# Sigmoid attention with a GELU feed-forward layer: raw weights and a parked intermediate move to GpSimd's DMA queue, three loads move to the next stage, and the first stage decodes one weight unit less

## The chip, the cores and the metric

One core of a Trainium2 chip runs the kernel. The metric is the device time of one execution in microseconds (us).

## The reference

```
scores = q @ k^T / 8 - ln(448)             # 8 batches, 12 heads, 448 tokens, 64 channels
x = sigmoid(scores) @ v                     # laid out as [8*448 tokens, 12*64 = 768 channels]
h = x @ w_in                                # w_in 768 x 2048
out = (0.5 * h * (1 + erf(h / sqrt(2)))) @ w_out   # w_out 2048 x 768
```

Everything is float32 at the interface except the two weight matrices, which lie in DRAM as 64-bit floats: the kernel turns them into 32-bit floats itself ("decodes" them).

## The kernel before

**Batches and tokens.** The eight batches are taken in the order 7, 0, 1, ... 6. The attention output of the first one is parked in DRAM (`scr_x`), and its 448 tokens are dealt out, 64 each, to the seven others. So the feed-forward layer runs seven times over 512 tokens (448 + 64).

**Stages.** `attention_first` computes the first two batches' attention, 12 head pairs, with nothing else for TensorE. Then come seven rounds of `ffn1(t)` (the first product, GELU) and `window(t + 2, t)`, in which the second product of round t is interleaved with the attention of a later batch. The first three batches ("plain", `PLAIN = 3`) multiply 32-bit floats directly; later ones and all feed-forward products use float32r, each operand split into a high and a low part (`xh`/`xl`, `whl`, `g`).

**Order.** The schedule is written out by hand: an engine executes its instructions in the order in which the program issues them, and a DMA queue issues its transfers in that order too. Each of SyncE's (`nc.sync`) and GpSimd's (`nc.gpsimd`) instruction streams is one such queue.

**A plain head pair n.** `load_plain(n)` issues four transfers on SyncE's queue, 704 KB in all: q (224 KB), k in two halves (112 KB each), v (256 KB). In `attention_first` pair n + 3 is loaded after the values of pair n - 1, into buffers that earlier pairs have left. `scores_plain` issues two score products (L340) for each of four key chunks and a sigmoid on ScalarE (L314) after each; `values_plain` multiplies with v (L356), copies the result (ScalarE L365) and subtracts (VectorE L366). For the first batch the two results go to `scr_x` (L368, L369) on SyncE's queue.

**Decoding.** `decoder()` is a generator that is advanced by `W.decode(n)`, n in chunks, two steps to a chunk. A chunk is one unit of w_in (768 KB raw) or half a unit of w_out (512 KB raw). `load(i)` fetches the raw chunk into one of three places in turn (two halves of `raw_ring`, one tile `raw`). Step one of iteration i runs `start(i)`: three VectorE instructions (L117, L119, L122) that wait for the raw load. Step two runs `scale(i)`: two ScalarE instructions (L130, L133), then for the chunk before it `end(i - 1)`: two VectorE instructions (L138, L147), and then `load(i + 2)`, which goes into the place that L138 has just finished reading. With L117, L119 and L138 all in program order between the sigmoids and casts of the attention, a late raw chunk holds VectorE, then ScalarE (L130), and then the sigmoid for which TensorE waits.

The pace of decoding is set by three numbers of chunks: `PACE_A` over `attention_first`, `PACE_F` over `ffn1(0)`, `PACE_W` over `window(2, 0)`. There are 40 chunks (16 of w_in, 24 of w_out). The call in the first stage is

```
for c in range(4):
    scores_plain(n, c)
    W.decode(PACE_A * (4 * n + c - 3) / (4 * total - 4))     # total = 12
```

Decoded w_in units are stored on SyncE's queue during `ffn1(0)` and decoded w_out units on GpSimd's (L190), for the later rounds to read back.

Of the kernel before, what the change touches and what calls it, by code (L numbers as in the profile page):

```python
# [9 lines left out]
F32 = mybir.dt.float32  # L10
# [3 lines left out]
I64 = mybir.dt.int64  # L14
# [8 lines left out]
def tile_sigmoid_attention_gelu_ffn(  # L23
# [11 lines left out]
    nc = tc.nc  # L35
    B, NPAIR, _, S = q.shape
# [28 lines left out]
    def g_tile(fc, name, dtype=F32R):  # L65
        return const.tile([P, 2, T], dtype, tag=f"g{fc}", name=name)
# [3 lines left out]
    scr_x = tc.dram_tile([2, P, NPAIR, S], F32, name="scr_x")  # L70
# [1 line left out]


    PLAIN = 3
    PACE_A, PACE_F, PACE_W = 14, 8, 24
    SUB_IN, SUB_OUT = NC * P, NFH * P // 2
    SUB = max(SUB_IN, SUB_OUT)
    KEPT = 4
# [5 lines left out]
    def width(kind):  # L84
        return (NC if kind == "in" else NFH) * P

    def decoder():


        chunks = [  # L90
            (kind, u, c0, sub)
            for kind, u in UNITS
            for sub in (SUB_IN if kind == "in" else SUB_OUT,)
            for c0 in range(0, width(kind), sub)
        ]
        raws, parts = {}, {}
        raw_ring = sb.tile([P, 2, 2 * SUB], U32, tag="raw", name="raw_ring", bufs=1)
        me_ring = sb.tile([P, 2, 2, SUB], U32, tag="me", name="me_ring", bufs=1)

        def load(i):  # L100
            if i >= len(chunks):
                return
            kind, u, c0, w = chunks[i]
            src = (w_in if kind == "in" else w_out)[u].rearrange("p a b -> p (a b)")
            if i % 3 < 2:
                raw = raw_ring[:, i % 3]
            else:
                raw = sb.tile([P, 2 * SUB], U32, tag="a", name=f"raw{i}", bufs=1)
            raw = raw[:, : 2 * w]
            nc.sync.dma_start(raw.bitcast(I64), src[:, c0 : c0 + w])  # L110
            raws[i] = raw.rearrange("p (n t) -> p n t", t=2)

        def start(i):
            w = chunks[i][3]
            low, high = raws[i][:, :, 0], raws[i][:, :, 1]
            m, e = me_ring[:, i % 2, 0, :w], me_ring[:, i % 2, 1, :w]
            nc.vector.tensor_scalar(e, high, 0x7FF00000, None, op0=ALU.bitwise_and)  # L117

            nc.vector.tensor_scalar(  # L119
                m, high, 11, 0x80000000, op0=ALU.logical_shift_left, op1=ALU.bitwise_or  # L120
            )
            nc.vector.scalar_tensor_tensor(  # L122
                m, low, 21, m, op0=ALU.logical_shift_right, op1=ALU.bitwise_or
            )
            parts[i] = m, e

        def scale(i):

            e = parts[i][1]
            nc.scalar.activation(  # L130
                e.bitcast(F32), e.bitcast(I32), AF.Relu, bias=1151.0 * 2**23, scale=-8.0
            )
            nc.scalar.activation(e, e.bitcast(F32), AF.Relu, bias=255.0 * 2**23, scale=-1.0)  # L133

        def end(i):
            high = raws.pop(i)[:, :, 1]
            m, e = parts.pop(i)
            nc.vector.scalar_tensor_tensor(  # L138
                e, high, 0x80000000, e, op0=ALU.bitwise_and, op1=ALU.bitwise_or
            )  # L140
            kind, u, c0, w = chunks[i]
            if c0 == 0 and kind == "in":
                first_w[kind, u] = g_tile(u, f"w_in{u}", F32).rearrange("p a b -> p (a b)")
            elif c0 == 0:
                first_w[kind, u] = sb.tile([P, WU], F32, tag="wst", name=f"w_out{u}", bufs=WST)
            t = first_w[kind, u][:, c0 : c0 + w]
            nc.vector.scalar_tensor_tensor(  # L147
                t, m, 2.0**-31, e.bitcast(F32), op0=ALU.mult, op1=ALU.mult
            )

        load(0)
        load(1)
        yield False
        for i in range(len(chunks) + 1):
            if i == 0:
                load(2)
            if i < len(chunks):
                start(i)
                yield False
                scale(i)  # L160
            if i > 0:
                end(i - 1)
                load(i + 2)
            yield i > 0 and chunks[i - 1][2] + chunks[i - 1][3] == width(chunks[i - 1][0])
# [77 lines left out]
    def rows(j):  # L242
        return slice(j * D, j * D + D)
# [72 lines left out]
    def load_plain(n):  # L316

        b, hp = divmod(n, NPAIR)
        if b >= PLAIN:
            return  # L320
        if n % 3 < 2:
            qk = sb.tile([P, 2, S], F32, tag="kr", name=f"qk{n}")
            qr, kr = qk[:, 0], qk[:, 1]
        else:
            qr, kr = (sb.tile([P, S], F32, tag="qr", name=f"{x}r{n}") for x in "qk")
        nc.sync.dma_start(qr, q[(b - 1) % B, hp])
        for j in range(2):
            nc.sync.dma_start(kr[rows(j)], k[(b - 1) % B, hp, rows(j), j])  # L328
        vr = sb.tile([P, 2, 4, D], F32, tag=("vr", "vs")[n % 2], name=f"vr{n}")
        nc.sync.dma_start(vr, v[(b - 1) % B, hp])  # L330
        raws[n] = qr, kr, vr
# [17 lines left out]
    def values_plain(n):  # L349
        b, hp = divmod(n, NPAIR)  # L350
        vr = raws.pop(n)[2]
        pav = ps_av.tile([P, 512], F32, tag="pav", name=f"pav{n}")
        for c in range(4):
            a = attn.pop((n, c))
            for j in range(2):
                nc.tensor.matmul(  # L356
                    pav[rows(j), :S], vr[:, j, c], a[:, j], start=c == 0, stop=c == 3
                )
        if b > 0:
            th, tl = xh[:, hp, :S], xl[:, hp, :S]  # L360
        else:
            th, tl = (
                sb.tile([P, S], F32R, tag="tmp", name=f"x{n}{b}_{hp}", bufs=3) for n in "hl"
            )
        nc.scalar.copy(th, pav[:, :S])  # L365
        nc.vector.tensor_tensor(tl, pav[:, :S], th, op=ALU.subtract)  # L366
        if b == 0:
            nc.sync.dma_start(scr_x[0, :, hp], th.bitcast(F32))  # L368
            nc.sync.dma_start(scr_x[1, :, hp], tl.bitcast(F32))  # L369

    def load_tokens(t):

        for n, x in enumerate((xh, xl)):
            nc.sync.dma_start(x[:, :, S:].bitcast(F32), scr_x[n, :, :, t * TOK : (t + 1) * TOK])
# [23 lines left out]
    def attention_first():  # L398

        total = 2 * NPAIR  # L400
        load_plain(0)
        load_plain(1)
        W.decode(0)
        load_plain(2)
        for n in range(total):
            for c in range(4):
                scores_plain(n, c)
                W.decode(PACE_A * (4 * n + c - 3) / (4 * total - 4))
            if n > 0:
                values_plain(n - 1)  # L410
            load_plain(n + 3)
            if n == NPAIR + 2:
                load_tokens(0)
            W.prepare_to(min(n - total + 3, 2))
        values_plain(total - 1)
# [17 lines left out]
    def ffn1(b):  # L433
        for fc in range(NF):
            if b == 0:
                W.store_to(fc + 3)
            if (b, fc) not in phs:
                hidden(b, fc, range(NC - 1))
            W.prepare_to(W.pos[b, "in", fc] + (2 if b == 0 else AHD))
            ph = hidden(b, fc, range(NC - 1, NC))  # L440
            if b == 0:
                W.prepare_to(W.pos[b, "in", fc] + 3)
            g[fc] = g_tile(fc, f"g{b}_{fc}")
            gf = sb.tile([P, T], F32, tag="tmp", name=f"gf{b}_{fc}", bufs=3)
            nc.scalar.activation(gf, ph, AF.Gelu)  # L445
            nc.scalar.activation(g[fc][:, 0], ph, AF.Gelu)  # L446
            nc.vector.tensor_tensor(g[fc][:, 1], gf, g[fc][:, 0], op=ALU.subtract)  # L447
            if b > 0:
                W.prepare_to(W.pos[b, "in", fc] + AHD + 1)
            if b + 2 >= PLAIN:  # L450
                if fc in (NF - 10, NF - 8):
                    load_pair(b + 2, (fc - NF + 10) // 2)
                if fc in (NF - 4, NF - 2):
                    split_head(b + 2, (fc - NF + 4) // 2)
                if fc == NF - 1:
                    load_pair(b + 2, 2)
            if b == 0:
                W.decode(PACE_A + PACE_F * (fc + 1) / NF)
# [83 lines left out]
    with psum("ps_sc1", 2) as ps_sc, psum("ps_av1", 2) as ps_av:  # L542
        ffn1(0)
        window(2, 0)
    ps_sc, ps_av = (ctx.enter_context(psum(*pool)) for pool in (("ps_sc", 1), ("ps_av", 4)))
    for t in range(1, NB):
        ffn1(t)
        window(t + 2, t)
# [33 lines left out]
```

## Time and profile before

| | |
|---|---|
| time, median of 3 runs | 1219.84 us (1219.82 to 1221.88) |
| the profiled execution's own time | 1225.91 us |
| its span, first to last instruction | 1224.1 us |
| TensorE busy | 1210.4 us (99%) |
| ScalarE, VectorE, GpSimd busy | 815.5, 769.2, 8.6 us |
| first stage (`attention_first`) | up to 92 us |
| `ffn1(0)` | 92 to about 157 us |
| `window(2, 0)` | about 157 to 262 us |

The busy time of an engine is the sum of its instructions; matmul ends are modelled, so TensorE's busy share doesn't show how full it is, but a gap between its instructions is real idle time. The profiled execution lasted 6.07 us longer than the median of the runs without a profile.

### The profile page before, as it was taken

The page shows a single profiled execution, that of the slowest core. Times are in us where ns is not written, and L with a number is a line of the kernel's source. Part 1 is how long each engine was busy: PE and PEld are TensorE (multiplying, and loading weights), DVE is VectorE, ACT ScalarE, POOL GpSimd, SP SyncE. Part 2 cuts the span into 40 slices and gives each one's busy share as a digit, 9 for nine tenths or more (in the row PEclk, how much of TensorE's full clock was granted, in tenths as well). Part 3 has the DMA queues.
Part 4 walks back from the last instruction along what each step waited for, and adds up shares of the span by engine and source line. Part 5 has one row for each costly group of instructions (what it writes and reads, how often), then busy time and mean ns, then how long its engine had stood idle before and what let it go on. Part 6 is the DMA issues. An engine that isn't in the chain of part 4 may idle for free.

```text
span 1224.1 us, 15057 instructions
## 1 busy us (share of the span) xinstructions
PE 1210.4 (99%) x5448; PEld 961.8 (79%) x5448; DVE 769.2 (63%) x1127; ACT 815.5 (67%) x1247; POOL 8.6 (1%) x18
## 2 busy tenths in 40 slices
PE   8999999999999999999999999999999999999998
PEld 4338866668888888888888888888888888888887
DVE  4777788623589734798445896447984378953420
ACT  7886576534699744899546997459984489954421
POOL 0000000000000000000000000000000000000000
PEclk9999999999999999999999999999999999999999
DMA  8994567524443135442244432345422544223330
GB/s 278 300 283 153 183 214 246 183 82 154 154 140 113 57 104 174 150 143 73 91 157 147 142 108 76 123 145 162 133 69 87 172 148 147 78 82 104 131 114 26
DMA packets 79881, 172.23 MB, mean 141 GB/s; under 512 B 24256, under 2 KB 39616, under 8 KB 79808
## 3 DMA queue, kind: packets, MB, share of 16 engines
q1 hardware_dynamic: 78080, 164.99, 42.4%
q0 software_dynamic: 1728, 6.29, 1.3%
q8 instruction: 43, 0.70, 0.2%
q14 instruction: 30, 0.25, 0.1%
HBM read 144.90 MB, written 26.35 MB: 140 GB/s over the span
## 4 chain that ended last, share of the span: by engine, by line
PE 95%; DMA 3%; DVE 1%; ACT 1%; SPq 0%; issue 0%; DVEq 0%; ACTq 0%
PE po L477 13%; PE po L478 13%; PE po L479 12%; PE ph L428 12%; PE ph L429 12%; PE ph L430 12%; PE pav L386 7%; PE sc L294 6%; PE pav L356 3%; PE sc L340 3%; DMA raw_ring<-w_in_dram 1%; PE sc_l L289 1%; DMA raw<-w_in_dram 1%; DMA qr<-q_dram 1%; DVE me_ring L117 0%; SPq L328 0%
## 5 line engine op out<-in xcount | busy, mean ns | idle before, releaser
L477 PE MATMUL po<-g,whl 128*128 128x512 f32 x672 | 263.3, 392 | 0.0
L478 PE MATMUL po<-g,whl 128*128 128x512 f32 x672 | 262.3, 390 | 0.0
L479 PE MATMUL po<-g,whl 128*128 128x512 f32 x672 | 261.9, 390 | 0.0
L428 PE MATMUL ph<-xh,whl 128*128 128x512 f32 x672 | 261.5, 389 | 0.0
L429 PE MATMUL ph<-xl,whl 128*128 128x512 f32 x672 | 261.4, 389 | 0.0
L430 PE MATMUL ph<-xh,whl 128*128 128x512 f32 x672 | 261.4, 389 | 0.0
L227 DVE TENSOR_TENSOR whl<-wst,whl 128x768 fp32r<-128x768 f32 (+1 forms) x168 | 179.6, 1072 | 65.1 <-ACT whl L226 61.9
L447 DVE TENSOR_TENSOR g<-gf,g 128x512 fp32r<-128x512 f32 x112 | 77.5, 692 | 212.0 <-ACT g L446 211.8
L445 ACT ACTIVATE gf<-ph 128x512 f32<-128x512 f32 x112 | 66.9, 597 | 199.4 <-PE ph L430 185.5
L226 ACT CAST whl<-wst 128x768 fp32r<-128x768 f32 (+1 forms) x168 | 155.4, 928 | 5.5 <-PE po L479 4.2
L477 PEld LDWEIGHTS po<-g,whl 128*128 128x128 f32 x672 | 126.2, 188 | 31.9 <-issue 8.1
L428 PEld LDWEIGHTS ph<-xh,whl 128*128 128x128 f32 x672 | 126.1, 188 | 26.9 <-issue 0.7
L479 PEld LDWEIGHTS po<-g,whl 128*128 128x128 f32 x672 | 126.1, 188 | 26.8
L430 PEld LDWEIGHTS ph<-xh,whl 128*128 128x128 f32 x672 | 126.1, 188 | 26.2
L429 PEld LDWEIGHTS ph<-xl,whl 128*128 128x128 f32 x672 | 126.1, 188 | 26.1
L478 PEld LDWEIGHTS po<-g,whl 128*128 128x128 f32 x672 | 126.2, 188 | 23.8
L314 ACT ACTIVATE a<-sc 128x896 f32<-128x896 f32 (+1 forms) x174 | 128.3, 786 | 17.3 <-PE sc L340 8.3
L308 DVE TENSOR_TENSOR al<-a,ah 128x896 fp32r<-128x896 f32 x120 | 97.8, 855 | 35.4 <-ACT ah L307 35.4
L307 ACT CAST ah<-a 128x896 fp32r<-128x896 f32 x120 | 85.7, 754 | 5.6 <-PE pav L386 4.2
L386 PE MATMUL pav<-ah,vs 128*128 128x448 f32 x240 | 87.7, 365 | 0.0
L294 PE MATMUL sc<-qs,ks 128*128 128x448 f32 x360 | 82.9, 366 | 0.0
L294 PEld LDWEIGHTS sc<-qs,ks 128*128 128x128 f32 x360 | 67.6, 188 | 6.8
(60 smaller groups left out, 1210.4 us busy)
## 6 DMA issues: line engine op xcount, KB each, us to landing
wst<-scr_in SPq DMA_DIRECT2D x96, 384.0 KB, 3.1
wst<-scr_out SPq DMA_DIRECT2D x72, 512.0 KB, 3.3
kr<-k_dram SPq DMA_DIRECT2D x30, 448.0 KB, 4.3
vr<-v_dram SPq DMA_DIRECT2D x48, 256.0 KB, 4.6
out_dram<-ob SPq DMA_DIRECT2D x42, 224.0 KB, 2.0
raw_ring<-w_in_dram SPq DMA_DIRECT2D x11, 768.0 KB, 7.0
raw_ring<-w_out_dram SPq DMA_DIRECT2D x16, 512.0 KB, 4.7
qr<-q_dram SPq DMA_DIRECT2D x36, 224.0 KB, 3.2
```

Source lines behind the costliest of these rows:

```text
L226: nc.scalar.copy(hl[:, 0, :w], t[:, :w])
L227: nc.vector.tensor_tensor(hl[:, 1, :w], t[:, :w], hl[:, 0, :w], op=ALU.subtract)
L294: nc.tensor.matmul(o, ks[:, keys], qs, start=n == 0, stop=n == 1)
L308: nc.vector.tensor_tensor(al[t][:, c], a[t][:, c], ah[t][:, c], op=ALU.subtract)
L314: nc.scalar.activation(a, sc, AF.Sigmoid, bias=NEG_LOG_S, scale=SCALE)
L386: nc.tensor.matmul(pav[:, :S], vs[:, j, c], a, start=n == 0, stop=n == len(terms) - 1)
L428: nc.tensor.matmul(ph, wl, xh[:, cc], start=cc == 0, stop=False)
L429: nc.tensor.matmul(ph, wh, xl[:, cc], start=False, stop=False)
L430: nc.tensor.matmul(ph, wh, xh[:, cc], start=False, stop=cc == NC - 1)
L477: nc.tensor.matmul(po, wl, g[fc][:, 0], start=first, stop=False)
L478: nc.tensor.matmul(po, wh, g[fc][:, 1], start=False, stop=False)
L479: nc.tensor.matmul(po, wh, g[fc][:, 0], start=False, stop=last)
```

## The change

- Raw weight chunks (L110) are issued on GpSimd's queue instead of SyncE's; so are the two stores of the parked first batch (L368, L369).
- In `attention_first` pairs 12, 13 and 14 (the third batch's first three) are not loaded any more; `ffn1(0)` loads them after feature chunks 1, 3 and 5.
- `PACE_A` goes from 14 to 13 chunks and `PACE_F` from 8 to 8.5, so the first stage decodes one chunk less and the window begins half a chunk behind where it began.

```diff
-    PACE_A, PACE_F, PACE_W = 14, 8, 24
+    PACE_A, PACE_F, PACE_W = 13, 8.5, 24
...
-            nc.sync.dma_start(raw.bitcast(I64), src[:, c0 : c0 + w])
+            nc.gpsimd.dma_start(raw.bitcast(I64), src[:, c0 : c0 + w])
...
         if b == 0:
-            nc.sync.dma_start(scr_x[0, :, hp], th.bitcast(F32))
-            nc.sync.dma_start(scr_x[1, :, hp], tl.bitcast(F32))
+            nc.gpsimd.dma_start(scr_x[0, :, hp], th.bitcast(F32))
+            nc.gpsimd.dma_start(scr_x[1, :, hp], tl.bitcast(F32))
...
             if n > 0:
                 values_plain(n - 1)
-            load_plain(n + 3)
+            if n + 3 < total:
+                load_plain(n + 3)
...
             if b > 0:
                 W.prepare_to(W.pos[b, "in", fc] + AHD + 1)
+            if b == 0 and fc % 2 == 1 and fc < 6:
+                load_plain(2 * NPAIR + fc // 2)
```

## Rows read from the trace of the kernel before

**Rows 1.** The profile's page: its first line and the busy time of the engines.

```profile
span 1224.1 us, 15057 instructions
...
PE 1210.4 (99%) x5448; PEld 961.8 (79%) x5448; DVE 769.2 (63%) x1127; ACT 815.5 (67%) x1247; POOL 8.6 (1%) x18
```

**Rows 2.** Busy time by stretch of the span: stretch in us, its length, then for each engine busy us and (instructions), the granted clock of TensorE, the share of the DMA engines' time, GB/s.

```profile
5.00:26.00 21.00, 20.20 (x92) 10.09 (x89) 10.10 (x14) 17.36 (x22) 0.00 (x0) 1.00 0.93 304
26.00:50.00 24.00, 23.96 (x120) 9.35 (x122) 17.63 (x25) 20.62 (x26) 0.00 (x0) 1.00 0.92 299
50.00:62.00 12.00, 9.21 (x46) 3.23 (x42) 9.50 (x14) 9.59 (x13) 0.00 (x0) 1.00 0.93 295
62.00:78.00 16.00, 16.00 (x84) 6.08 (x80) 11.70 (x16) 14.52 (x19) 0.00 (x0) 1.00 1.05 302
78.00:92.00 14.00, 11.65 (x51) 3.97 (x49) 10.53 (x14) 9.25 (x13) 0.00 (x0) 0.88 0.80 262
92.00:157.00 65.00, 65.00 (x289) 53.84 (x288) 47.11 (x68) 38.35 (x61) 1.20 (x2) 1.00 0.49 173
157.00:262.00 105.00, 105.00 (x471) 65.59 (x469) 70.10 (x114) 63.09 (x87) 5.61 (x10) 1.00 0.58 184
262.00:1220.00 958.00, 958.00 (x4309) 808.69 (x4308) 592.43 (x864) 640.65 (x1007) 0.00 (x0) 1.00 0.38 120
```

**Rows 3.** The timeline of TensorE in the first stage: start, length, engine and line, operation, count, and in brackets the idle time before it and what ended that. The rows at 36.51, 42.88 and 75.14 are from stretches without a gap, for comparison.

```profile
4.10 8.71 PE L340 MATMUL sc<-qk 64*128 64x448 f32 x32 [4.10 <-DMA qk<-k_dram]
...
26.04 1.02 PE L340 MATMUL sc<-qk 64*128 64x448 f32 x4 [0.84 <-ACT a L314]
...
36.51 3.28 PE L340 MATMUL sc<-qr,kr 64*128 64x448 f32 x16
...
42.88 3.28 PE L340 MATMUL sc<-qk 64*128 64x448 f32 x16
...
54.04 1.02 PE L340 MATMUL sc<-qk 64*128 64x448 f32 x4 [2.27 <-ACT a L314]
...
61.46 1.02 PE L340 MATMUL sc<-qr,kr 64*128 64x448 f32 x4 [0.35 <-ACT a L314]
...
75.14 2.48 PE L356 MATMUL pav<-a,vr 128*64 128x448 f32 x12
...
83.17 1.74 PE L340 MATMUL sc<-qr,kr 64*128 64x448 f32 x4 [2.35 <-ACT a L314]
84.84 3.41 PE L356 MATMUL pav<-a,vr 128*64 128x448 f32 x12
...
91.94 0.50 PE L428 MATMUL ph<-xh,whl 128*128 128x512 f32 x1
```

**Rows 4.** The chain that ended last, in the first stage: start us, us, what.

```profile
15.40 6.79 DMA raw<-w_in_dram
...
51.04 0.44 SPq L330
51.58 5.11 DMA raw<-w_in_dram
...
71.02 7.59 DMA raw_ring<-w_in_dram
```

**Rows 5.** The timeline of VectorE (same columns), where it waits for raw weights, and the end of the chunk before.

```profile
48.01 0.94 DVE L138 SCALAR_TENSOR_TENSOR me_ring<-raw,me_ring 128x768 uint32<-128x768 uint32 x1
48.99 0.96 DVE L147 SCALAR_TENSOR_TENSOR w_in<-me_ring 128x768 f32<-128x768 uint32 x1
...
54.10 0.62 DVE L366 TENSOR_TENSOR xl<-pav,xh 128x448 fp32r<-128x448 f32 x1
56.78 0.56 DVE L117 TENSOR_SCALAR me_ring<-raw 128x768 uint32<-128x768 uint32 x1 [2.06 <-DMA raw<-w_in_dram]
57.25 0.55 DVE L119 TENSOR_SCALAR me_ring<-raw 128x768 uint32<-128x768 uint32 x1
...
78.70 0.56 DVE L117 TENSOR_SCALAR me_ring<-raw_ring 128x768 uint32<-128x768 uint32 x1 [1.66 <-DMA raw_ring<-w_in_dram]
```

**Rows 6.** The DMA issues of the first 92 us: what, queue, form and count, KB each, median us from issue to landing; the first line is the sum.

```profile
DMA packets 12183, 26.38 MB, mean 287 GB/s; under 512 B 2953, under 2 KB 8321, under 8 KB 12177
...
raw_ring<-w_in_dram SPq DMA_DIRECT2D x11, 768.0 KB, 7.0
...
raw<-w_in_dram SPq DMA_DIRECT2D x5, 768.0 KB, 6.8
```

**Rows 7.** The timeline of SyncE's queue (same columns).

```profile
48.96 1.37 SPq L328 DMA_DIRECT2D kr<-k_dram  x2
50.43 1.05 SPq L330 DMA_DIRECT2D vr<-v_dram  x1
51.58 0.38 SPq L110 DMA_DIRECT2D raw<-w_in_dram  x1
...
72.66 0.40 SPq L326 DMA_DIRECT2D qk<-q_dram  x1
```

**Rows 8.** The DMAs that GpSimd issues in the kernel before: one of its timeline, and from the list of DMA issues of the whole span the landing of that transfer and of one other of the same size on SyncE's queue.

```profile
205.50 0.62 POOL L190 DMA_DIRECT2D scr_out<-w_out  x1 [9.59 <-DVE w_out L147]
...
raw_ring<-w_out_dram SPq DMA_DIRECT2D x16, 512.0 KB, 4.7
...
scr_out<-w_out POOLq DMA_DIRECT2D x12, 512.0 KB, 4.3
```

## The prediction

> **What bounds the kernel now.** I read the page first, for the busy shares. TensorE is busy for 1210.4 of the 1224.1 us, the next engine for 815.5 [rows 1]. So only TensorE's gaps, or stretches in which it runs slower than it can, are worth anything. The table of windows says where they are: after 92 us TensorE is busy in all of every stretch (65.00 of 65, 105.00 of 105, 958.00 of 958), but not in 50 to 62 and in 78 to 92, where the granted clock also falls to 0.88 [rows 2]. In that first stage the DMA engines are busy for 0.80 to 1.05 of the time and move 262 to 304 GB/s [rows 2], after it for about half the time: it is the one stage in which transfers compete.
>
> Next I read TensorE's timeline there. A head pair without gaps takes 6.37 us (from 36.51 to 42.88), so 12 pairs need 76.4 us; the stage runs from 4.10 to 91.94, that is 87.8 us, 11.4 too many [rows 3]. The excess has three parts [rows 3]:
> - gaps: 0.84 at 26.04, 2.27 at 54.04, 0.35 at 61.46, 2.35 at 83.17, in sum 5.81 us, all waits for a sigmoid;
> - slow products behind the last gap: 4 score products in 1.74 instead of 1.02, 12 value products in 3.41 instead of 2.48, in sum 1.65 us. Their stretch has the 0.88 clock, the others have 1.00 [rows 2];
> - about 4 us left, most of it at the start (32 score products in 8.71, where 16 take 3.28), where the first loads come in.
>
> The chain of waits then tells what the sigmoids were late for: transfers of raw weights, issued at 15.40, 51.58 and 71.02 [rows 4]. VectorE's timeline shows the same from the other side: L117 starts at 56.78 after 2.06 us idle, and at 78.70 after 1.66, each time released by a raw chunk [rows 5]. ScalarE waits for that instruction (L130 stands before the next sigmoid in its program), TensorE for the sigmoid. So the removable part is 5.81 + 1.65 = 7.46 us, and its cause is raw chunks that land late.
>
> **The budget of a raw chunk.** In the schedule one decode call goes with each of a pair's four key chunks, every 6.37 / 4 = 1.59 us. With PACE_A = 14 a chunk takes 44 / 14 calls = 5.0 us; with 13 it takes 5.4 us. A load goes out in the second step of one iteration and is read in the first step of the iteration after next: three steps, 1.5 chunks. That allows 7.5 us before and 8.1 us after. The median landing is 7.0 us in the ring and 6.8 in the third place [rows 6]: half a microsecond of slack, and the chunk issued at 71.02 took 7.59 [rows 4]. This is why the stage stalls at some chunks only.
>
> **The change, part by part.**
> *Raw loads on GpSimd's queue.* The chunk behind the 54.04 gap could have been issued at 48.95, when L138 ended [rows 5]; on SyncE's queue it stood behind a pair's loads and went out at 51.58 [rows 4, 7]. Without these 2.6 us it lands at about 54.1 instead of 56.7; VectorE is free for it at 54.7 [rows 5]. So the gap of 2.27 and its echo of 0.35 go: 2.62 us.
>
> What does issuing from GpSimd cost? Raw loads on that queue are not in this trace; the nearest rows are its stores of w_out units, 512 KB each: 0.62 us to issue, and a landing of 4.3 us, where 512 KB of raw weights on SyncE's queue take 4.7 [rows 8]. Below: nothing, even 0.4 gained. Above: the whole 0.62 added. I take 0.3 us per chunk, inside the 0.6 us by which the budget grows. GpSimd has no other work (8.6 us in the whole span [rows 1]), so nothing of its own is queued behind a waiting load.
>
> The Trainium skill speaks against this part: in "SBUF — State Buffer", section "SBUF: two separate sides", a DMA issued from GpSimd can't get its descriptors written while VectorE runs an instruction in a two-port mode, and `tensor_scalar` can enter one. Rows: L117 and L119 together last from 56.78 to 57.80, 1.0 us for 2 x 768 elements, against 0.96 for one L147 [rows 5], so they do run in a fast mode; but L147 stands between L138, which frees the place, and the next L117, and 0.62 us of issuing fits into its 0.96. The w_out stores are issued where L117 follows at once, and land in 4.3 us [rows 8], so no row shows the lock. By the rule the worst case is 1.0 us more per chunk.
>
> *The parked batch's stores* (12 transfers of 224 KB) follow on the same queue. They stay behind the same raw loads as before and lose the pair's loads in front of them: nothing, either way below 1 us, since `tmp` has three buffers and the next use is a pair (6.37 us) later.
>
> *One chunk less.* It takes 786 KB and, with the three pairs (2.16 MB), 2.95 of the stage's 26.38 MB away; at 287 GB/s that is 10.3 of 92 us of transfers [rows 6]. The DMA engines then need about 82 us, less than the 83 at which the products could end (4.10 + 76.4 + the start's excess). That decode work falls to `ffn1(0)` and the window, where TensorE has no gap and VectorE is busy for 47.11 of 65 and 70.10 of 105 us [rows 2]. There the decoder is still ahead of the product: when the window first asks for a w_out unit (20 chunks finished), its pace has brought it to 21, and it gains from there (24 chunks to the window, of which the product takes 22). Cost nothing; if that cover were gone, half a chunk, about 2.5 us, once.
>
> *Three pairs' loads moved.* The first of them is issued at 72.66 [rows 7], while the chunk of 71.02 is in flight; 721 KB at 302 GB/s is 2.4 us, more than VectorE's 1.66 us of idleness at 78.70 [rows 2, 5]. So the gap at 83.17 should close, and with it the slow clock: 2.35 + 1.65 = 4.0; I leave 0.4, since ScalarE has a cast of weights to fit in there too: 3.6. In `ffn1(0)` the 12 issues cost SyncE some 2 us per pair behind stores that are needed three feature chunks later, and the DMA engines there are busy for 0.49 [rows 2]; the data is needed from 157 us. Nothing.
>
> *The start.* The third raw chunk, issued at 15.40 before [rows 4], is now issued at once, with nothing ahead of it but two others. That takes the gap at 26.04 away (0.84), but its 786 KB compete with the first three pairs: at 304 GB/s at most 2.6 us of delay [rows 2]; at least nothing. I take 1.0, since the third pair is not read before 16 us: together -0.2.
>
> Sum: 2.62 + 3.6 - 0.2 = 6.0 us, less 0.8 for gaps that reappear elsewhere: 5.2. Against the profiled execution's own 1225.91 this gives 1220.7.
>
> **From the profiled execution to the median.** The median, 1219.84, is 6.07 us shorter. After 92 us TensorE has no idle time to shorten, so part of these 6 us must be gaps of the first stage that undisturbed runs don't have. At worst all of it: then 7.46 - 6.07 = 1.4 us are left to gain. At best none: 5.2. I take two thirds, 3.5 us: 1219.84 - 3.5 = 1216.3.
>
> **The rivals.**
> *A: nothing to measure.* The stage's transfers are shared by the same engines, whichever queue they come from, and the undisturbed runs have only small gaps. For it: the 6.07 us above, and DMA shares around 0.93 [rows 2], which a new queue doesn't lower. Against: 2.95 MB do leave. Result: 1.4 us gained or less, or lost as much, 1218.4 to 1221.2. Also here: raw chunks that take their share of the DMA engines at once and delay the pairs' loads, so that TensorE waits for q and k instead; the start's 2.6 us price against a gain of 3.5. The Trainium skill's "DMA: Bandwidth & Descriptors", section "Queues, rings and completion order", says that each engine goes round between queues by packets; no row here shows two queues loaded at once.
> *B: slower.* GpSimd's queue delivers raw chunks later than the budget. The place is L117 in the first stage. At a landing of L the chunk takes L / 1.5; the stage ends where it did before when 13 chunks take 7.5 us longer than at 5.4 each, that is at 6.0 a chunk, a landing of 9.0 us. Beyond that it is slower: at 10 us 13 x (6.7 - 5.4) = 17 us against 7.5 removed, 9 us lost, 1229. For it: no raw load has been seen on that queue. Against: 4.3 us for 512 KB [rows 8], and it takes 2 us more than now. If each load had to wait for a whole L117 and L119, 1.0 us a chunk [rows 5], 7.0 would become 8.0, just inside the budget, and what is gained would shrink to rival A's 1.4 or less; half of A's chance at most is for this. It is the Trainium skill's rule from above.
>
> **How the numbers follow.** What a measurement of this kernel can tell from no change is about 0.2%, 2.4 us. The forecast (1212.5 to 1217.4) gets 0.56, rival A 0.29 (1217.4 to 1222.3), rival B 0.15. So faster 0.56, same 0.29, slower 0.15. The range goes from the whole 7.46 removed, 1212.5, to 1221.7, which takes in A; B's most part and a little of A's end stay out.
>
> **What the profile after would show.** Right: L117 without waits over 1 us from 20 us on, no TensorE gap over 1 us in the first stage, no stretch with a granted clock under 1.00, the first L428 at 85 to 88 us, raw landings on GpSimd's queue at 7 us or less. Wrong: landings over 9 us, or TensorE waits released by q or k loads, or a first L428 no earlier with the idle time moved to the start. If L428 comes 5 us earlier and the median stays, the profiled execution's gaps were its own.

## The result and the profile after

The changed kernel takes 1226.8 us in the median (1225.78 to 1228.74, 4 runs), the kernel before 1220.31 beside it: a ratio of 1.0053, interval 1.0035 to 1.0070. It is about 6.5 us slower, where 3.5 us less was predicted.

The two profiled executions do not show that: 1224.0 us of span after, 1224.1 before. The one of before, 1225.91 us in all, is longer than any other run of that kernel (1219.4 to 1225.8 in the comparisons below); the one of after, 1225.78, at the lower end of its kernel's. So the stages are compared, not the spans. Busy time by stretch, columns as in [rows 2]:

```profile
5.00:26.00 21.00, 19.47 (x72) 8.35 (x72) 7.74 (x12) 12.74 (x16) 1.64 (x3) 0.92 0.85 275
13.00:18.30 5.30, 4.90 (x15) 2.41 (x15) 0.02 (x1) 2.56 (x3) 0.00 (x0) 0.68 0.99 286
...
50.00:62.00 12.00, 12.00 (x64) 4.67 (x62) 9.96 (x14) 10.39 (x14) 2.22 (x5) 1.00 0.91 311
...
78.00:92.00 14.00, 14.00 (x71) 6.15 (x67) 10.38 (x14) 10.26 (x14) 1.05 (x2) 1.00 1.03 376
92.00:157.00 65.00, 64.35 (x285) 52.52 (x285) 49.40 (x70) 39.98 (x63) 5.15 (x10) 1.00 0.40 128
157.00:262.00 105.00, 104.35 (x468) 65.13 (x465) 70.42 (x115) 62.75 (x88) 14.56 (x28) 1.00 0.62 194
```

The stretches in which TensorE had its gaps, 50 to 62 and 78 to 92, are full now, and the last has a granted clock of 1.00 instead of 0.88 [rows 2]. The loss is in the first row: in 5 to 26 us TensorE issues 72 products instead of 92, and from 13 to 18.3 us its clock is 0.68, so it ran partly at 1.2 and not 2.4 GHz. And the two stretches after 92 us, which had no idle time, have 0.65 us each. From the first feed-forward product to the end of the span it is 1134.4 us now and 1132.2 before, 2.2 us more. TensorE's timeline (columns as in [rows 3]; L429 is L428 of before, L480 is L477):

```profile
4.41 6.47 PE L340 MATMUL sc<-qk 64*128 64x448 f32 x16 [4.41 <-DMA qk<-k_dram]
11.81 0.99 PE L340 MATMUL sc<-qk 64*128 64x448 f32 x2 [0.93 <-DMA qk<-k_dram]
13.40 4.97 PE L340 MATMUL sc<-qk 64*128 64x448 f32 x14 [0.60 <-DMA qk<-k_dram]
18.30 2.48 PE L356 MATMUL pav<-a,vr 128*64 128x448 f32 x12
...
37.16 1.02 PE L340 MATMUL sc<-qk 64*128 64x448 f32 x4 [0.45 <-ACT a L314]
...
76.08 1.02 PE L340 MATMUL sc<-qk 64*128 64x448 f32 x4 [0.45 <-ACT a L314]
...
89.62 0.50 PE L429 MATMUL ph<-xh,whl 128*128 128x512 f32 x1
...
102.81 0.47 PE L429 MATMUL ph<-xh,whl 128*128 128x512 f32 x1 [0.65 <-DVE whl L227]
...
209.23 0.50 PE L480 MATMUL po<-g,whl 128*128 128x512 f32 x1 [0.65 <-DVE whl L227]
```

The first 32 score products end at 18.37 (13.40 + 4.97), against 12.81 (4.10 + 8.71) [rows 3]: 5.6 us late. TensorE waits twice there for the k of the second pair, until 11.81 and until 13.40. From 18.30 on only two gaps of 0.45 are left, and the first feed-forward product comes at 89.62, where it was 91.94. So the middle of the stage got shorter, as was predicted, and its beginning longer.

What GpSimd's queue does at the start (columns as in [rows 7]):

```profile
2.31 1.20 POOL L110 DMA_DIRECT2D raw_ring<-w_in_dram  x2
3.50 0.53 POOL L110 DMA_DIRECT2D raw<-w_in_dram  x1
```

All three first chunks, 2.36 MB, are issued by 4.0 us. Before, the first two left at 5.31, behind two pairs' loads and ahead of the third pair's, and the third at 15.40, behind four pairs' [rows 4]. SyncE's queue before:

```profile
3.53 1.11 SPq L328 DMA_DIRECT2D qk<-k_dram  x2
...
5.31 0.91 SPq L110 DMA_DIRECT2D raw_ring<-w_in_dram  x2
6.26 0.43 SPq L326 DMA_DIRECT2D qr<-q_dram  x1
```

The DMA queues between 4 and 11 us, as packets, MB and share of the engines' time, first after, then before:

```profile
q0 software_dynamic: 338, 1.88, 70.1%
q1 hardware_dynamic: 419, 0.69, 28.4%
```

```profile
q1 hardware_dynamic: 803, 2.29, 94.5%
```

With two queues loaded, GpSimd's takes 70% of the engines' time with 338 packets and SyncE's 28% with 419. The counts are nearer to even than the bytes, because a packet of raw weights holds 5.6 KB on average against 1.6 KB. The pairs' loads get 0.69 MB through in these 7 us.

### The profile page after: what moved, and what is told of

Its sections match the earlier page's. It is cut to its first block, busy times and chain, and to the rows that moved or that the text cites. A ratio compares the mean times of both kernels' runs of the same rounds, so it can differ in the third digit from the quotient of the medians.

```text
span 1224.0 us, 15076 instructions
## 1 busy us (share of the span) xinstructions
PE 1211.9 (99%) x5448; PEld 960.9 (79%) x5448; DVE 769.0 (63%) x1127; ACT 815.0 (67%) x1247; POOL 36.7 (3%) x70
## 4 chain that ended last, share of the span: by engine, by line
PE 92%; DMA 3%; DVE 2%; ACT 2%; issue 1%; SPq 0%; POOL 0%; DVEq 0%; POOLq 0%; ACTq 0%
PE ph L429 12%; PE ph L431 12%; PE ph L430 12%; PE po L480 12%; PE po L481 12%; PE po L482 12%; PE pav L386 7%; PE sc L294 6%; PE pav L356 4%; PE sc L340 3%; DMA raw<-w_out_dram 1%; PE sc_l L289 1%; DMA raw_ring<-w_out_dram 1%; DMA qk<-k_dram 1%; DVE whl L227 1%
## 5 line engine op out<-in xcount | busy, mean ns | idle before, releaser
L480 PE MATMUL po<-g,whl 128*128 128x512 f32 x672 | 263.4, 392 | 0.7 <-DVE whl L227 0.7
L429 PE MATMUL ph<-xh,whl 128*128 128x512 f32 x672 | 261.6, 389 | 0.7 <-DVE whl L227 0.7
L227 DVE TENSOR_TENSOR whl<-wst,whl 128x768 fp32r<-128x768 f32 (+1 forms) x168 | 179.5, 1071 | 65.2 <-ACT whl L226 62.0
L480 PEld LDWEIGHTS po<-g,whl 128*128 128x128 f32 x672 | 126.2, 188 | 33.0 <-issue 8.1
L429 PEld LDWEIGHTS ph<-xh,whl 128*128 128x128 f32 x672 | 126.1, 188 | 27.7 <-ACT g L447 1.0
```

Of the source, the lines that this page charges most:

```text
L227: nc.vector.tensor_tensor(hl[:, 1, :w], t[:, :w], hl[:, 0, :w], op=ALU.subtract)
L429: nc.tensor.matmul(ph, wl, xh[:, cc], start=cc == 0, stop=False)
L480: nc.tensor.matmul(po, wl, g[fc][:, 0], start=first, stop=False)
```

## The experiments

Each was timed beside the kernel before, on the same chip.

**The kernel before, profiled once more (e0).**

> The kernel before, unchanged, profiled once more. Its profiled execution took 1225.91 us where its other runs took 1219.8 to 1221.9. Theory: the gaps of 5.8 us and the 1.65 us of slow clock in the first stage belong to that one execution; another one ends its first stage at about 86 to 88 us instead of 91.9 and spans about 1218 to 1220. Rival: the gaps are always there, the stage ends at 91 to 92 again, and the 6 us lie elsewhere.

1221.41 us, a span of 1219.6. TensorE's gaps in the first stage:

```profile
25.41 1.02 PE L340 MATMUL sc<-qk 64*128 64x448 f32 x4 [0.46 <-ACT a L314]
...
53.39 1.02 PE L340 MATMUL sc<-qk 64*128 64x448 f32 x4 [2.25 <-ACT a L314]
...
80.31 1.02 PE L340 MATMUL sc<-qr,kr 64*128 64x448 f32 x4 [1.19 <-ACT a L314]
...
87.43 0.50 PE L428 MATMUL ph<-xh,whl 128*128 128x512 f32 x1
```

The gaps at 25, 53 and 80 us are there again, but sum to 3.9 us instead of 5.81, and none is followed by slow products: the stage ends at 87.43. From there to the end it is 1132.2 us in both executions (1219.6 - 87.43 and 1224.1 - 91.94). So the 4.5 us between these two lie entirely in the first stage, and about half of what I took for removable, slow products with the lower clock among it, belonged to that one execution.

**The first three raw chunks back on SyncE's queue (e1).**

```diff
-            nc.gpsimd.dma_start(raw.bitcast(I64), ...)
+            (nc.sync if i < 3 else nc.gpsimd).dma_start(raw.bitcast(I64), ...)
```

> The changed kernel, but the first three raw chunks are issued on SyncE's queue in their old places behind the pairs' loads; all later ones stay on GpSimd's. Theory (three raw chunks issued at 2.3 to 4.0 us take the DMA engines from the second pair, which starts 5.6 us late): the first 32 score products end at about 13 us instead of 18.4, the stage ends near 84 to 85, and the time falls by about 5 us to 1221 to 1222. Rival (the loss lies in the later stages, or raw chunks on GpSimd's queue are slow throughout): the time stays at 1225 to 1227.

1220.39 us in the median, a little less than I gave, ratio 0.9992 (0.9980 to 1.0004); the changed kernel's was 1.0053.

```profile
4.04 8.44 PE L340 MATMUL sc<-qk 64*128 64x448 f32 x32 [4.04 <-DMA qk<-k_dram]
12.40 2.48 PE L356 MATMUL pav<-a,vr 128*64 128x448 f32 x12
...
31.27 1.02 PE L340 MATMUL sc<-qk 64*128 64x448 f32 x4 [0.45 <-ACT a L314]
...
84.04 0.50 PE L429 MATMUL ph<-xh,whl 128*128 128x512 f32 x1
...
97.25 0.47 PE L429 MATMUL ph<-xh,whl 128*128 128x512 f32 x1 [0.65 <-DVE whl L227]
```

The values begin at 12.40, a gap of 0.45 is what is left in the middle, and the stage ends at 84.04, 5.6 us earlier than in the changed kernel. The 0.65 at 97.25 stays; it belongs to the paces (e4). With three transfers out of forty back on SyncE's queue, no loss against the kernel before is left. The profiled execution is the fastest of its runs (1219.06).

**All raw chunks back on SyncE's queue (e2).**

```diff
-            nc.gpsimd.dma_start(raw.bitcast(I64), ...)
+            nc.sync.dma_start(raw.bitcast(I64), ...)
```

> The changed kernel with all raw chunks back on SyncE's queue; the parked stores stay on GpSimd's, the three pairs' loads and the paces stay as changed. Theory (the start is what costs): as the run with only the first three back, 1221 to 1222, plus up to 2 us if the gap from a raw chunk behind a pair's loads comes back. Rival (the moved loads or the paces cost the time): 1225 or more.

1219.54 us, less than the 1221 to 1222 I gave, ratio 0.9975 (0.9967 to 0.9984): faster than before. The stage ends at 84.04 as well, and the gap at 53 us is not there, although each chunk again stands behind pairs' loads.

**Only the raw chunks' queue changed (e3).** The kernel before with that one line of the change.

> The kernel before with one edit: all raw chunks on GpSimd's queue. Theory (the start is what costs): 4 to 6 us slower than before, 1224 to 1226, with the second pair's first product at 13 to 14 us. Rival (the queue is neutral and the loads and paces cost): 1219 to 1221.

1228.95 us, above what I gave, ratio 1.0053 (1.0038 to 1.0068), the same as for the whole change.

```profile
11.76 0.99 PE L340 MATMUL sc<-qk 64*128 64x448 f32 x2 [1.48 <-DMA qk<-k_dram]
...
56.67 1.02 PE L340 MATMUL sc<-qk 64*128 64x448 f32 x4 [0.46 <-ACT a L314]
...
83.83 1.02 PE L340 MATMUL sc<-qr,kr 64*128 64x448 f32 x4 [1.42 <-ACT a L314]
...
90.94 0.50 PE L428 MATMUL ph<-xh,whl 128*128 128x512 f32 x1
```

The wait for the second pair's k is there (1.48 at 11.76), with the paces and loads of before, and so is the gap of the old pace at 83.83. The gap near 54 us is down to 0.46, with the old pace and the stores where they were. The stage ends 3.5 us later than in e0. This execution, 1224.94, was 3.3 us faster than any other run of the kernel, so it shows only a part of the loss.

**One part taken back at a time, from e2.** The expectations first:

```diff
e4: PACE_A, PACE_F, PACE_W = 13, 8, 24        (instead of 13, 8.5, 24)
e5: load_plain(n + 3) for every n again, none in ffn1
e6: scr_x stores on nc.sync again
e7: PACE_A, PACE_F, PACE_W = 14, 8, 24        (as before)
```

> The run with all raw chunks on SyncE's queue, with PACE_F = 8 instead of 8.5 (13, 8, 24). Theory (8.5 makes the first decode call of ffn1 take two steps, whose five VectorE and two ScalarE instructions stand before the next weight split, and TensorE waits 0.65 us at 97 us): the first call takes one step, that gap goes, the time falls by about 1 us to 1218.5, and the window, which begins half a chunk further behind, shows no gap. Rival (the half chunk is needed): a new gap in the window, 1219.5 or more.

> The run with all raw chunks on SyncE's queue, with the three pairs loaded in attention_first again (paces 13, 8.5, 24; parked stores on GpSimd's queue). Theory (the moved loads closed the gap at 80 us, where a pair's loads fly beside a raw chunk): a gap of 1 to 2 us near 77 to 80 us again, 1220.5 to 1221.5. Rival (the pace alone gives raw chunks enough time): no gap, 1219.5.

> The run with all raw chunks on SyncE's queue, with the parked stores on SyncE's queue as well: of the change only the moved loads and the paces are left. Theory (the parked stores' queue is neutral): 1219.5 within 0.7 us. Rival (it is the stores on another queue that close the gap at 53 us, where a raw chunk stood behind them and a pair's loads): the gap of 2.3 us returns, 1221.5.

> The run with all raw chunks on SyncE's queue, with the paces of before (14, 8, 24). Theory (the pace gives each raw chunk 8.1 us instead of 7.5 and so closes the gap at 53 us, though the chunks still stand behind the pairs' loads): the gap of about 2.3 us returns, the gap at 97 us goes, 1220.5 to 1221. Rival (the parked stores and the moved loads did it): no gap at 53 us, 1218.5.

| | time us | ratio to before | first feed-forward product at | from there to the end of the span |
|---|---|---|---|---|
| e2 | 1219.54 | 0.9975 (0.9967 to 0.9984) | 84.04 | 1133.5 |
| e4 | 1218.76 | 0.9973 (0.9963 to 0.9983) | 84.94 | 1132.5 |
| e5 | 1219.89 | 0.9982 (0.9973 to 0.9990) | 84.50 | 1133.4 |
| e6 | 1219.95 | 0.9986 (0.9977 to 0.9995) | 85.96 | 1133.1 |
| e7 | 1220.18 | 0.9991 (0.9982 to 1.0001) | 85.31 | 1132.5 |

The last column is the later stages alone. With PACE_F = 8.5 it is 0.6 to 1.0 us longer; with 8 the gap near 97 us is absent and nothing appears in the window (e4). In the timeline of VectorE after that gap looks like this (the changed kernel):

```profile
97.30 0.69 DVE L448 TENSOR_TENSOR g<-gf,g 128x512 fp32r<-128x512 f32 x1 [1.44 <-ACT g L447]
97.91 0.55 DVE L117 TENSOR_SCALAR me_ring<-raw_ring 128x768 uint32<-128x768 uint32 x1
98.38 0.55 DVE L119 TENSOR_SCALAR me_ring<-raw_ring 128x768 uint32<-128x768 uint32 x1
98.97 0.96 DVE L122 SCALAR_TENSOR_TENSOR me_ring<-raw_ring,me_ring 128x768 uint32<-128x768 uint32 x1
99.85 0.95 DVE L138 SCALAR_TENSOR_TENSOR me_ring<-raw_ring,me_ring 128x768 uint32<-128x768 uint32 x1
100.83 0.96 DVE L147 SCALAR_TENSOR_TENSOR w_in<-me_ring 128x768 f32<-128x768 uint32 x1
101.71 0.95 DVE L227 TENSOR_TENSOR whl<-w_in,whl 128x768 fp32r<-128x768 f32 x1
```

Five decoding instructions stand between a GELU difference and the weight split of L227, where in the kernel before the call took one step, the three of L117, L119 and L122: at 13 + 8.5 / 16 the step count rounds up to two.

For the gaps of the first stage, e5, e6 and e7 say which part is needed for which (TensorE's timeline, e5, then e6, then e7):

```profile
71.02 1.02 PE L340 MATMUL sc<-qk 64*128 64x448 f32 x4 [0.45 <-ACT a L314]
```

```profile
33.23 1.02 PE L340 MATMUL sc<-qk 64*128 64x448 f32 x4 [1.66 <-ACT a L314]
```

```profile
51.28 1.02 PE L340 MATMUL sc<-qk 64*128 64x448 f32 x4 [0.46 <-ACT a L314]
...
78.20 1.02 PE L340 MATMUL sc<-qr,kr 64*128 64x448 f32 x4 [1.18 <-ACT a L314]
```

With the loads back there is no gap at 77 to 80 us: the slower pace closes it without them. With the old pace, and stores and loads as changed, the gap at 51 us is down to 0.46, while 1.18 us remain at 78. With the old stores, the largest is 1.66 at 33 us, and none is left near 53 or 80. So the parts overlap: the gap at 53 us goes with the slower pace (e6), with the parked stores off SyncE's queue (e7), or with the raw chunks off it (e3), and the one at 80 us needs the pace. None of these runs has the pace alone. The theory of e6 came out in time (1219.5 was given), though not without a new gap; those of e5 and e7 (1 to 2 us and 2.3 us of gap back) did not. Of e4's theory the trace shows the gap gone and the later stages 1.0 us shorter, but the gain in time is not shown: the intervals of e2, e4, e5 and e6 overlap, and their ratios differ by at most 0.0013.

**Why the start is late (e8, e9).** Two edits of the changed kernel:

```diff
-            nc.gpsimd.dma_start(raw.bitcast(I64), ...)
+            (nc.scalar if i < 3 else nc.gpsimd).dma_start(raw.bitcast(I64), ...)    # e8
+            (nc.gpsimd if i < 1 else nc.sync).dma_start(raw.bitcast(I64), ...)      # e9
```

> The changed kernel, but the first three raw chunks are issued on ScalarE's queue, as early as GpSimd issued them (they have a queue of their own again, but one of the same kind as SyncE's); later ones stay on GpSimd's. Theory A (what costs is that three chunks are in flight early, beside the second pair's loads, whatever the queue): the first 32 score products end at 17 to 19 us again, 1225 to 1227. Theory B (what costs is GpSimd's queue itself, whose packets of 5.6 KB on average take 70% of the bytes from 4 to 11 us against 1.65 KB for a packet of SyncE's): packets of one size share evenly, the products end at 14 to 16 us, 1221 to 1224.

> The changed kernel with only the first raw chunk on GpSimd's queue, all later ones on SyncE's. Theory (the delay is the bytes that overtake the second pair's loads): one chunk of 786 KB instead of three, about a third of the 5.6 us, the first 32 score products end at 13.5 to 15 us, 1220.5 to 1222.5. Rival (any transfer on GpSimd's queue at the start costs a fixed delay): 17 to 18.5 us, 1225.

e8: 1224.5 us, ratio 1.0018 (1.0009 to 1.0027). e9: 1220.14 us, ratio 0.9983 (0.9974 to 0.9993). ScalarE's issues of raw chunks in e8, then TensorE's timeline and the DMA queues, first of e8 (4 to 9 us, by when its first two raw chunks had landed but for a few small packets; q10 is ScalarE's), then of e9 (SyncE's queue, 4 to 11 us):

```profile
0.92 0.86 ACTq L110 DMA_DIRECT2D raw_ring<-w_in_dram  x2
16.07 0.34 ACTq L110 DMA_DIRECT2D raw<-w_in_dram  x1
```

```profile
7.87 10.41 PE L340 MATMUL sc<-qk 64*128 64x448 f32 x32 [7.87 <-DMA qk<-k_dram]
18.21 2.48 PE L356 MATMUL pav<-a,vr 128*64 128x448 f32 x12
```

```profile
q10 hardware_dynamic: 229, 1.24, 75.4%
q1 hardware_dynamic: 235, 0.38, 26.3%
```

```profile
4.63 8.65 PE L340 MATMUL sc<-qk 64*128 64x448 f32 x32 [4.63 <-DMA qk<-k_dram]
13.22 2.48 PE L356 MATMUL pav<-a,vr 128*64 128x448 f32 x12
```

```profile
q1 hardware_dynamic: 720, 1.74, 71.1%
```

On ScalarE's queue two chunks left at 0.9 us, 1.4 earlier than on GpSimd's, and held up the first pair as well (7.87 instead of 4.41). The third left only at 16.07, behind sigmoids, so this start is that of two chunks issued earlier, and not of three issued as early as on GpSimd's. The values begin at 18.21, as late as after. The packets are as large there (1.24 MB in 229) and take 75% of the engines' time, so neither the late start nor the packets' size needs GpSimd's queue. This is theory A's start, not B's.

The time is not theory A's: 0.5 us below what it gave, and by the ratios (1.0018 and 1.0053, with intervals apart) the late start cost less here than in the changed kernel. The granted clock over the whole execution differs too: 0.999 to 1.000 in all ten runs of e8, 0.997 in three of the four of the changed kernel, 0.996 to 0.998 in five of the six of e3. The one other run of each of these two, at 0.999, is the profiled one and the fastest. A clock lower by 0.002 over 1224 us is 2.4 us, by estimate; so by that a part of the loss in time would be the clock, and the profiled executions show less of it than the others had. No run separates the two.

With one chunk instead of three, the values begin at 13.22, 0.8 us later than in e1, but within the 12.29 to 13.68 of the runs that have all first chunks on SyncE's queue (e1, e2, e4 to e7): no fixed cost of the queue, and less than a third of 5.6. From 4 to 11 us SyncE's queue moves 1.74 MB, at most 0.79 of it a raw chunk, so the pairs' loads get at least 0.95 MB through, against 0.69. The delay grows faster than the bytes.

**The third pair ahead of the first raw chunks (e10).** An edit of e4:

```diff
-        W.decode(0)
         load_plain(2)
+        W.decode(0)
```

> The run with all raw chunks on SyncE's queue and the paces 13, 8, 24, with the third pair's loads issued ahead of the first two raw chunks. Theory (the start is paced by ScalarE's eight sigmoids of 0.92 us, not by loads any more): the first 32 products end within 0.5 us of 13 us, the time stays at 1218.8 within 0.7 us. Rival (the third pair's loads are still late at the start): up to 1 us less, 1217.8.

1219.74 us, ratio 0.9983 (0.9974 to 0.9993), no better than e4 and 0.2 us above what the theory allowed; the first 32 products end at 13.2 us, as it said. This order gives nothing more.

## Why the prediction was wrong

The forecast had 0.56, slower by any way 0.15. **The start** is the term that failed. I took 1.0 us of delay and "at most 2.6", from the 786 KB of the third chunk. But the edit also moved the first two chunks ahead of the second pair's loads, which had stood before them on SyncE's queue, and the third ahead of the second, third and fourth pairs': 2.36 MB, which at 304 GB/s are 7.8 us by estimate, and not 2.6 [rows 2]. Measured are 5.6 us, part of it in the stretch with the 0.68 clock, and more clock was lost in the runs without a profile (e8). Rival A named this mechanism, pairs' loads delayed so that TensorE waits for k, but priced it with the same 2.6 us. The rule that I placed there, of the Trainium skill's "DMA: Bandwidth & Descriptors", section "Queues, rings and completion order", agrees with the counts so far as these can tell (338 against 419 packets for 1.88 against 0.69 MB). They are not always even: in e8 it was 152 against 98 from 4 to 7 us and 77 against 137 from 7 to 9.

**The size of the removable part** was read from one execution. 7.46 us were there; e0 has 3.9. The prediction saw that 6.07 us had to be explained and kept two thirds of the gain. What e2 and e4 gained, 0.25 to 0.27% or about 3 us, is near the forecast's 3.5, but this is luck: its terms were not the ones that came.

**The gaps of the middle** did close, to 0.45 each, and the clock of the last stretch rose to 1.00. Other signs that were named did not come: L117 still waits up to 1.86 us, the first product comes at 89.62 and not at 85 to 88, and landings in the third place are 7.8 us. The 2.62 us for GpSimd's queue rest on a wrong reading. The chunk issued at 51.58 landed at 56.7, and the gap of 2.27 had ended at 54.04, so it can have caused only the small gaps behind it, 0.35 at 61.46 the largest. VectorE before that gap, and SyncE's issue of the chunk that it waited for longest:

```profile
45.52 0.56 DVE L117 TENSOR_SCALAR me_ring<-raw_ring 128x768 uint32<-128x768 uint32 x1 [3.09 <-DMA raw_ring<-w_in_dram]
...
50.30 0.56 DVE L117 TENSOR_SCALAR me_ring<-raw_ring 128x768 uint32<-128x768 uint32 x1 [0.36 <-DMA raw_ring<-w_in_dram]
```

```profile
37.00 0.33 SPq L110 DMA_DIRECT2D raw_ring<-w_in_dram  x1
```

That chunk left as soon as its place was free (L138 ended at 36.97) and took 8.5 us to land: what was late was the landing, and not the place in the queue. The gap closes with the raw chunks on GpSimd's queue alone (e3), but e3 also starts 5 us late; and with the chunks back on SyncE's queue it stays closed (e2), where the budget is 8.1 us instead of 7.5 and the parked stores have left the queue: median landings are 6.0 us (ring) and 5.5 (third place) in e2, from 7.0 and 6.8 [rows 6], and 7.4 in the ring with the stores back (e6).

**GpSimd's queue in itself** was priced at 0.3 us a chunk. Median landings after are 6.8 and 7.8 us in the first stage; e1 and e2, which differ only in the later chunks' queue, both end the stage at 84.04, and their intervals in time overlap. Rival B, landings over 9 us, did not come: only the third chunk of the start took longer, 10.2 us, and it was not read before 24.6. The change is slower, but not by that. A lock-out by VectorE (the Trainium skill's "SBUF — State Buffer", section "SBUF: two separate sides") can't be told from these runs: raw chunks take 0.53 to 0.67 us to issue, where the stores had 0.62 [rows 8]. In `window(2, 0)` VectorE waits 9.8 us for raw chunks in e1 and 6.6 in e2, TensorE in neither; in the profile after it is 12.5 us, and there the gap at 209.23 follows. The cause of that gap is open: e1 and e3, with later chunks on GpSimd's queue too, don't have it.

**The decode work moved on**, "cost nothing", cost about 1 us (1133.1 to 1133.5 against 1132.5 in the table): not by its amount but by how the steps round, at one call of `ffn1`.

**The moved loads** cost nothing in `ffn1`, as predicted, and closed nothing that stayed open without them (e5).

The best version found is e4, or e2 within the uncertainty: the change without the move of the raw chunks (in e4 with `PACE_F` = 8), faster than before by 0.27% (0.17 to 0.37).

## What to carry to other kernels

A transfer that is moved to an idle queue is moved ahead of everything that stood before it in the old one: list those transfers with their bytes, above all at the start, where nothing covers a delay. Order within one queue was a priority: without it the start was 5.6 us later here. A chunk that lands after a gap has ended can't be its cause: read the times of both. Before a gap in a profile is priced, look whether that execution took as long as the others; and when a pace changes by a fraction, count the steps that each call takes.

## What the runs showed of the hardware

Between two loaded queues the packets were nearer to even than the bytes (338 to 419 for 1.88 to 0.69 MB in the profile after, 229 to 235 for 1.24 to 0.38 MB in e8). The packets of raw weights held 5.4 to 5.6 KB against 1.6 KB, and their queue took 70% of the engines' time against 28% in the profile after. TensorE's granted clock was 0.68 from 13 to 18.3 us after two waits for loads; in e8, where it waited until 7.87 us and then not again, it was 1.00 in the same stretch.
